# Linear attention and two MLPs on one Trainium2 core: the key-value products of two head pairs in one PSUM tile

## The chip, the cores and the metric

The kernel runs on one core of a Trainium2 chip. The metric is the device time of one execution in microseconds (us); lower is better. Several executions of the kernel before were timed, and one more was recorded by the hardware profiler.

## What is computed

Linear attention, and behind it two MLPs, all in float32 in and out:

```
kv  = einsum('bhsd,bhse->bhde', k, v)         # 8 batches, 8 heads, 576 x 64
o   = einsum('bhsd,bhde->bhse', q, kv)
o   = o / sqrt(mean(o*o, -1) + 1e-6) * g_norm
x   = o, heads side by side: 4608 tokens x 512
x   = leaky_relu(x @ w_in_1) @ w_out_1        # 512 -> 2048 -> 512
out = relu(x @ w_in_2)**2 @ w_out_2
```

## The kernel before

**Stages.** The tokens are nine blocks of 512. The first product of the first MLP (`gemm1`, L522) goes over block j and over m = 0 to 15, a column strip of 128 of the hidden layer: twelve matmuls of 128x512 each into one of four PSUM banks, as each operand is a high and a low part. One such (j, m) is called a slot here; there are 144, numbered 16*j + m. The attention of block j + 1 is done in the slots of block j. The other three products come after that, in a second, longer stage which the change doesn't touch.

**Order.** The order of the work is written out by hand: a list `prog` of steps is made first (L767 to L939) and then played (L993), and each step issues its instructions in that order on its engines, which run them in order. `attention_steps` (L498) gives the steps of a block to slots. For each head pair p (two heads, 0 to 3) it has `kv` (the product of a batch), `a` (the transpose of q, tile `qtps`), `b` (q times kv, tile `ops`), `s` and `t` (sums of squares, tile `ssps`), `c` and `d` (the norm). From block 2 on the head pairs stand four slots apart, and behind a pair's `a` come its `b` two slots later, `s` four, `t` and `c` five and `d` six slots later; `kv` has the slot of `a`. In a slot the steps on weights come first, then the eviction `leaky` of the slot before (L537, which also sends out stores that are due, `tick`, L242), then `gemm1`, then the attention.

**The product of one head pair** is `do_kv` (L349): ten matmuls (five chunks of the sequence, three of 128 rows and two of 96, for two heads) of 64x64 into the two diagonal quarters of a PSUM tile 128 wide, `kvps`. The trace has two rows of each, one per pass. Two copies on ScalarE (L371) then take the high part to the tile `kv`, and two subtractions on VectorE (L374) the low part. Batch 0 is done ahead of slot 0 (L367); batches 1 to 7 make 28 such steps. Six `kv` tiles are used in turn.

**Loads.** `load_kv` (L334) takes two tiles, for k and v of a head pair, and issues four DMAs on the queue of SyncE. `pump` (L976) issues loads ahead of need: a list of `kv` and weight loads, in the order in which the program uses them, goes out as long as at most ten tiles (`LD_BUFS`) are held; `kv` takes two, a weight one, and the head of the list holds up what is behind it. The tiles come free at the step `kv` or `join`.

**Tiles.** Nearly all large tiles come from one list of 44 (`take_big`, `give_big`, L130): the oldest free one is taken. A tile that is sent to DRAM is given back when its store is issued (L242), so the next user's first write waits until that DMA has landed. Such stores are the prepared weights (`whS`, `whA` and others, written on ScalarE at L269 and on GpSimd at L270), and they share the queue of SyncE with all loads.

**PSUM in the attention.** `at_tile` (L327) gives banks 4 to 7 in turn while `gemm1` uses 0 to 3.

Of the kernel before, what the change touches and what calls it, by code (L numbers as in the profile page):

```python
# [11 lines left out]
F32R = mybir.dt.float32r  # L12
U32 = mybir.dt.uint32
AF = mybir.ActivationFunctionType
ALU = mybir.AluOpType
# [3 lines left out]
def tile_linear_attention_two_mlps(  # L19
# [26 lines left out]
    nc = tc.nc  # L46
    B, H, S, D = q.shape
# [6 lines left out]
    P = 128  # L54
    KC = DM // P
    NM = DFF // P
    NP = H // 2

    SCH = ((P, 3), (96, 2))
    SC = sum(n for _, n in SCH)  # L60
# [5 lines left out]
    LD_BUFS, Q_BUFS, KV_BUFS = 10, 4, 6  # L66
# [27 lines left out]
    const = ctx.enter_context(tc.tile_pool(name="const", bufs=1))  # L94
# [7 lines left out]
    ps = ctx.enter_context(tc.tile_pool(name="ps", bufs=1, space=bass.MemoryType.PSUM))  # L102
    dram = ctx.enter_context(tc.tile_pool(name="dram", bufs=1, space=bass.MemoryType.DRAM))

    f32 = lambda t: t.bitcast(F32)
# [4 lines left out]
    eps = const.tile([P, 1], F32, name="eps")  # L110
    eps2 = const.tile([P, 1], F32, name="eps2")
    gneg = const.tile([P, 1], F32, name="gneg")
    kv_t = [const.tile([P, 2, P], F32R, name=f"kv{n}") for n in range(KV_BUFS)]
    x2_d = [dram.tile([KC, P, TB], F32, name=f"x2_{n}") for n in range(NT // TB)]


# [13 lines left out]
    def take_big(shape, dtype, name):  # L130
        n = big_free.pop(0)
        return big.tile(shape, dtype, tag=f"s{n}", name=name), n

    def give_big(*ns):
        big_free.extend(ns)
# [4 lines left out]
    def psum(n, name):  # L140
        return ps.tile([P, TB], F32, tag=f"b{n}", name=name)
# [176 lines left out]
    kv_raw = {}  # L318
# [8 lines left out]
    def at_tile(w, name):  # L327

        at_n[0] += 1
        return psum(at_n[0] % 8 if spare else 4 + at_n[0] % 4, name)[:, :w]  # L330

    x_t = {}

    def load_kv(b, p):  # L334
        tiles = []
        for n, x in enumerate((k, v)):
            name = f"{'kv'[n]}_raw{b}_{p}"
            a, slot = take_big([P, 2, SC, D], F32, name)
            t0 = c0 = 0
            for r, c in SCH:  # L340
                (nc.scalar if n and b == 0 and p else nc.sync).dma_start(
                    out=a[:r, :, c0:c0 + c, :].rearrange("p h c d -> p h (c d)"),
                    in_=x[b, 2 * p:2 * p + 2, t0:t0 + r * c].rearrange("h (p c) d -> p h (c d)", c=c),
                )
                t0, c0 = t0 + r * c, c0 + c
            tiles.append((a, slot))
        kv_raw[b, p] = tiles

    def do_kv(b, p):  # L349
        (kt, k_slot), (vt, v_slot) = kv_raw.pop((b, p))  # L350
        ps = at_tile(P, f"kvps{b}_{p}")
        for c, n in enumerate(n for n, times in SCH for _ in range(times)):
            for h in range(2):
                r = slice(h * D, (h + 1) * D)
                nc.tensor.matmul(
                    out=ps[r, r],
                    lhsT=kt[:n, h, c, :],
                    rhs=vt[:n, h, c, :],
                    start=(c == 0),
                    stop=(c == SC - 1),  # L360
                )
        give_big(k_slot, v_slot)
        t = kv_t[(b * NP + p) % KV_BUFS]
        if b == 0:
            for h in range(2):
                r = slice(h * D, (h + 1) * D)
                nc.vector.tensor_copy(out=kvf_t[p][r, r], in_=ps[r, r])  # L367
            return
        for h in range(2):
            r = slice(h * D, (h + 1) * D)  # L370
            nc.scalar.activation(out=t[r, 0, r], in_=ps[r, r], func=AF.Copy)  # L371
        for h in range(2):
            r = slice(h * D, (h + 1) * D)
            nc.vector.tensor_tensor(  # L374
                out=t[r, 1, r], in0=ps[r, r], in1=f32(t[r, 0, r]), op=ALU.subtract
            )

    def split_kv(p):
# [117 lines left out]
    kv_done = set()  # L496

    def attention_steps(j, pace, a, b_, s, c, d):  # L498
        steps = {}

        def add(n, *st):
            steps.setdefault(n, []).append(st)

        for p in range(NP):
            at0 = int(pace * p)
            for b in range(j * TB // S, (j * TB + TB - 1) // S + 1):
                if (b, p) not in kv_done:
                    kv_done.add((b, p))
                    add(at0 - (j == 0), "kv", b, p)
            add(at0 + a, "a", j, p)  # L510
            add(at0 + b_, "b", j, p)
            add(at0 + s, "s", j, p)
            add(at0 + c, "t", j, p)
            add(at0 + c, "c", j, p)
            add(at0 + d, "d", j, p)
        return steps
# [250 lines left out]
    with tc.manual_schedule():  # L767

        prog = [("const",), ("gn",), ("x", 0)]
        steps = attention_steps(0, 1, 0, 1, 2, 2, 3)  # L770
        jobs = [(0, m, 0) for m in range(NM)]
        for at0 in (3, 5, 6):
# [41 lines left out]
        for s, (j, m) in enumerate(slots):  # L814
            if m == 0 and j + 1 < NB:
                at0, pace = (s - 5, 4) if j else (s, 4)
                put(s, "x", j + 1)
                lags = (2, 4, 5, 6) if j else (1, 2, 2, 3)
                for n, sts in attention_steps(j + 1, pace, 0, *lags).items():
                    for st in sts:  # L820
                        put(at0 + n, *st)
# [44 lines left out]
        u = 0  # L866
        at_slot(t2 - 28, "cap", 21)
        at_slot(t2 - 27.9, "want", (1, 0), 0, NSLOT // 2)
        for x, (half, z) in enumerate(insts):
            t0 = t2 + NPR * u  # L870
            pairs = [(n,) for n in range(half * NPAIR // 2, (half + 1) * NPAIR // 2)]
            if len(SETS[z]) == 1:
                pairs = [pairs[0] + pairs[1], pairs[2] + pairs[3]]
            again = x + 1 < len(insts) and insts[x + 1][1] == z
            if not (x and insts[x - 1][1] == z):
# [4 lines left out]
                for y, (kind, name) in enumerate(todo):  # L880
                    at0 = t0 - lead + 0.7 * y
                    if kind in ("oh", "ol"):
                        nth = [PRODUCTS[p][1] for p in ORDER].index(name)
                        if nth >= EARLY:
                            at0 = max(at0, t0 - 6.6 + 2 * (nth - EARLY) + (0.8 if kind == "ol" else 0))
                    elif name == "T4":
                        at0 = t0 - lead + 0.7 * y
                        at0 = max(at0, t0 - 6.6 + 2 * (4 - EARLY) + 0.9)
# [10 lines left out]
            for y, mine in enumerate(pairs):  # L899
                free = y == len(pairs) - 1 and not again  # L900
                for n in range(NPR):
                    at0 = t2 + NPR * u + 2 * n
                    at_slot(at0, "f", u, z, mine, n, free)
                    c = {2: "C11", 5: "C22", 4: "C21", 3: "C12"}.get(ORDER[n])
# [44 lines left out]
        def drop_pairs(ps):  # L949
# [7 lines left out]

        do = {
            "const": constants, "gn": scale_g, "x": x_tiles, "kv": do_kv,
            "a": stage_a, "b": stage_b, "s": stage_s, "t": stage_t, "kvs": split_kv, "lo": relieve, "c": stage_c, "d": stage_d, "mlp": spare.clear,  # L960
            "scale": scale_w, "join": join_w, "w": split_w, "g1": gemm1, "lk": leaky,
# [3 lines left out]
        }  # L965
        load = {
            "kv": (load_kv, 0, 2), "scale": (load_w, 0, 1), "a": (load_q, 1, 1)
        }
        free_by = {"kv": "kv", "join": "scale", "a": "a"}
        free = [LD_BUFS, Q_BUFS]  # L970
        queue = [
            [(x, st) for x, st in enumerate(prog) if st[0] in load and load[st[0]][1] == n]
            for n in range(2)
        ]

        def pump():  # L976
            while True:
                n = min(
                    (n for n in range(2) if queue[n] and load[queue[n][0][1][0]][2] <= free[n]),
                    key=lambda n: queue[n][0][0], default=None,  # L980
                )
                if n is None:
                    break
                kind, *args = queue[n].pop(0)[1]
                free[n] -= load[kind][2]
                load[kind][0](*args)


# [1 line left out]
        nc.vector.memset(eps, EPS)  # L990
        nc.scalar.activation(out=eps2, in_=eps, func=AF.Abs_reciprocal_sqrt)
        pump()
        for kind, *args in prog:  # L993
            do[kind](*args)
            if kind in free_by:
                _, n, tiles = load[free_by[kind]]
                free[n] += tiles
                pump()


# [30 lines left out]
```

## Time and profile before

| | us |
|---|---|
| median of 3 timed runs (1619.87 to 1621.56) | 1620.13 |
| the profiled execution | 1621.47 |
| its span, first to last instruction | 1619.4 |
| TensorE busy | 1580.0 |
| VectorE busy | 1218.4 |
| ScalarE busy | 768.0 |
| GpSimd busy | 181.0 |

In the rows, PE is TensorE's matmuls, PEld its weight loads, DVE VectorE, ACT ScalarE, POOL GpSimd, and SPq the queue on which SyncE issues DMAs. `out<-in` names the tiles. A bracket at the end of a row gives the idle time of the engine ahead of it and what ended that. The stage with attention reaches from about 31 us (slot 0) to about 548 us.

### The profile page before, as it was taken

To read this page: it belongs to the slowest core of one execution; us is meant where nothing else is said; L and a number is where in the kernel's file an instruction comes from. 1 tells how busy PE (TensorE), PEld (TensorE's weight loads), DVE (VectorE), ACT (ScalarE), POOL (GpSimd) and SP (SyncE) were. 2 spreads that over 40 slices of the span, in tenths; PEclk is the share of its full clock that TensorE was granted. 3 is DMA by queue.
4 is the path that set the end of the run, shared out by engine and by line. 5 is a ranking of instruction groups with operands and counts; after the bars stand their busy time and mean duration, and the time that the engine had idled before them with its cause. 6 is when DMAs were issued, how large, how long until landed. Compare 5 with 4: busy or idle time off the path is not lost. (4 is left out here: it accounts for less than half of the span.)

```text
span 1619.4 us, 27835 instructions
## 1 busy us (share of the span) xinstructions
PE 1580.0 (98%) x10500; PEld 1424.8 (88%) x10500; DVE 1218.4 (75%) x1912; ACT 768.0 (47%) x1435; POOL 181.0 (11%) x208
## 2 busy tenths in 40 slices
PE   5999999999999999999999999999999999999999
PEld 3788877887878899999999988888888999999998
DVE  5967877877773588887778777748886777777776
ACT  4756666565563344444444444534444344444443
POOL 0004444353442000000000000000000000000000
PEclk8999999999999999999999999999999999999999
DMA  9879999999869944444446654574459833344342
GB/s 231 254 210 283 336 288 314 293 301 345 300 232 328 363 132 132 131 131 131 130 132 226 224 177 160 181 255 155 157 169 348 309 130 131 131 131 131 130 133 83
DMA packets 248934, 338.44 MB, mean 209 GB/s; under 512 B 54752, under 2 KB 179680, under 8 KB 248800
## 3 DMA queue, kind: packets, MB, share of 16 engines
q1 hardware_dynamic: 247200, 335.78, 63.3%
q8 instruction: 83, 1.36, 0.3%
q10 hardware_dynamic: 1600, 0.89, 0.2%
q14 instruction: 51, 0.42, 0.1%
HBM read 198.18 MB, written 138.41 MB: 208 GB/s over the span
## 5 line engine op out<-in xcount | busy, mean ns | idle before, releaser
L527 PE MATMUL hps<-xh,w 128*128 128x512 f32 x1152 | 382.7, 400 | 10.5 <-ACT w L213 5.7
L527 PEld LDWEIGHTS hps<-xh,w 128*128 128x128 f32 x1152 | 218.3, 190 | 61.8 <-DVE w L214 6.9
L527 PE MATMUL hps<-xl,w 128*128 128x512 f32 x576 | 226.5, 393 | 0.0
L527 PEld LDWEIGHTS hps<-xl,w 128*128 128x128 f32 x576 | 109.6, 190 | 22.1 <-issue 1.0
L539 ACT ACTIVATE h<-hps 128x512 f32<-128x512 f32 x144 | 84.2, 589 | 20.6 <-DMA g<-h 16.0
L633 DVE TENSOR_TENSOR h_C<-aps,u 128x512 f32<-128x512 f32 x72 | 49.6, 688 | 45.1 <-PE aps L654 44.9
L633 DVE TENSOR_TENSOR u<-bps,p 128x512 f32<-128x512 f32 x72 | 49.5, 688 | 33.7 <-ACT p L664 20.8
L443 POOL TENSOR_TENSOR sqs<-sqo,sqs 128x512 fp32r<-128x512 f32 x28 | 43.3, 1547 | 189.6 <-DVE sqs L442 170.0
L664 ACT ACTIVATE p<-aps 128x512 f32<-128x512 f32 x36 | 21.3, 591 | 73.3 <-PE aps L654 73.3
L471 DVE SCALAR_TENSOR_TENSOR sqo<-ssps,sqo 128x512 f32<-128x512 f32 x36 | 24.9, 691 | 40.1 <-ACT sqo L470 39.8
L654 PE MATMUL aps<-op_B21h,w 128*128 128x512 f32 (+1 forms) x160 | 52.1, 375 | 1.1 <-ACT p L664 1.1
L654 PE MATMUL bps<-op_T4h,w 128*128 128x512 f32 (+1 forms) x160 | 51.3, 369 | 0.7 <-DVE u L633 0.7
L654 PE MATMUL aps<-op_B22h,w 128*128 128x512 f32 (+1 forms) x160 | 51.1, 368 | 0.0
L654 PE MATMUL bps<-op_T2h,w 128*128 128x512 f32 (+1 forms) x160 | 51.0, 368 | 0.0
L654 PE MATMUL bps<-op_T3h,w 128*128 128x512 f32 (+1 forms) x160 | 51.0, 368 | 0.0
L654 PE MATMUL aps<-op_B11h,w 128*128 128x512 f32 (+1 forms) x160 | 51.0, 368 | 0.0
L654 PE MATMUL aps<-op_T1h,w 128*128 128x512 f32 (+1 forms) x160 | 51.0, 368 | 0.0
L633 DVE TENSOR_TENSOR u<-ps,p 128x512 f32<-128x512 f32 x18 | 12.5, 692 | 50.9 <-ACT p L729 50.9
L671 ACT ACTIVATE h_C<-aps 128x512 f32<-128x512 f32 x36 | 21.6, 599 | 61.0 <-issue 31.1
L685 DVE SCALAR_TENSOR_TENSOR h_C<-h_C 128x512 f32<-128x512 f32 x72 | 49.1, 682 | 0.0
L181 DVE SCALAR_TENSOR_TENSOR w_raw<-w_raw 128x512 uint32<-128x512 uint32 x64 | 47.3, 739 | 2.2
L195 DVE SCALAR_TENSOR_TENSOR wt<-wt,w_raw 128x512 uint32<-128x512 uint32 x64 | 44.3, 693 | 2.2
(1417 smaller groups left out, 4174.4 us busy)
## 6 DMA issues: line engine op xcount, KB each, us to landing
g_raw<-g SPq DMA_DIRECT2D x144, 512.0 KB, 5.2
w<-w SPq DMA_DIRECT2D x84, 512.0 KB, 6.7
g<-h SPq DMA_DIRECT2D x144, 256.0 KB, 4.9
g<-h_C SPq DMA_DIRECT2D x144, 256.0 KB, 2.5
w_raw<-in_moe_w_in_dram SPq DMA_DIRECT2D x32, 512.0 KB, 5.3
w_raw<-in_moe_w_out_dram SPq DMA_DIRECT2D x32, 512.0 KB, 5.4
w<-whS SPq DMA_DIRECT2D x64, 256.0 KB, 4.7
x_raw<-x SPq DMA_DIRECT2D x32, 512.0 KB, 6.5
```

The lines of the kernel that those rows point to most:

```text
L181: nc.vector.scalar_tensor_tensor(out=lower, in0=lower, scalar=29, in1=upper, op0=ALU.logical_shift_right, op1=ALU.bitwise_or,)
L195: nc.vector.scalar_tensor_tensor(out=t, in0=t, scalar=3, in1=lower, op0=ALU.logical_shift_left, op1=ALU.bitwise_or,)
L443: nc.gpsimd.tensor_tensor(out=sqs[:, 1], in0=sqo[:, 0], in1=f32(sqs[:, 0]), op=ALU.subtract)
L471: nc.vector.scalar_tensor_tensor(out=z, in0=ps, scalar=EPS, in1=z, op0=ALU.add, op1=ALU.mult)
L527: nc.tensor.matmul(out=ps, lhsT=w[:, wh, c * P:(c + 1) * P], rhs=x_t[j][xh, c // 2][0][:, c % 2, :], start=(c == 0 and y == 0), stop=(c == ...
L539: nc.scalar.activation(out=h, in_=h_ps.pop((j, m)), func=AF.Prelu, alpha=0.01)
L633: nc.vector.tensor_tensor(out=t, in0=x, in1=y, op=ALU.add)
L654: nc.tensor.matmul(out=ps[:, p], lhsT=w[:, wh, c, :], rhs=t[xh][:, c, :], start=(fresh and p == 0 and c == 0 and y == 0), stop=(p == len(p ...
L664: nc.scalar.activation(out=p1, in_=ps, func=AF.Copy)
L671: nc.scalar.activation(out=h, in_=ps, func=AF.Relu)
L685: nc.vector.scalar_tensor_tensor(out=h, in0=h, scalar=0.0, in1=h, op0=ALU.max, op1=ALU.mult)
```

## The change

`do_kv` and `load_kv` take one or two head pairs. With two, the matmuls of both stand one after the other in one PSUM tile 256 wide, and each of the four copy-out instructions takes both pairs: 64 partitions by 2 x 64 elements. The two `kv` tiles become halves of one. The step has the slot of the first pair, so the second pair's product is made four slots earlier. Its load asks for four tiles at once and issues eight DMAs. Batch 0 and the first two pairs of batch 2 stay single. So 13 steps have two pairs and two have one, in place of 28.

```diff
-    kv_t = [const.tile([P, 2, P], F32R, name=f"kv{n}") for n in range(KV_BUFS)]
+    kv_g = [const.tile([P, 2, 2, P], F32R, name=f"kv{n}") for n in range(KV_BUFS // 2)]
+    kv_t = [kv_g[n // 2][:, n % 2] for n in range(KV_BUFS)]
...
-    def load_kv(b, p):
+    def load_kv(b, *pairs):
+        for p in pairs:
+            load_kv_pair(b, p)
+
+    def load_kv_pair(b, p):
...
-    def do_kv(b, p):
-        (kt, k_slot), (vt, v_slot) = kv_raw.pop((b, p))
-        ps = at_tile(P, f"kvps{b}_{p}")
...
+    def do_kv(b, *pairs):
+        ps = at_tile(P * len(pairs), f"kvps{b}_{pairs[0]}")
+        for u, p in enumerate(pairs):
+            (kt, k_slot), (vt, v_slot) = kv_raw.pop((b, p))
+            for c, n in enumerate(n for n, times in SCH for _ in range(times)):
+                for h in range(2):
+                    nc.tensor.matmul(
+                        out=ps[h * D:(h + 1) * D, u * P + h * D:u * P + (h + 1) * D],
+                        lhsT=kt[:n, h, c, :],
+                        rhs=vt[:n, h, c, :],
+                        start=(c == 0),
+                        stop=(c == SC - 1),
+                    )
+            give_big(k_slot, v_slot)
...
+        t = kv_g[(b * NP + pairs[0]) % KV_BUFS // 2][:, pairs[0] % 2:pairs[-1] % 2 + 1]
+        by_u = ps.rearrange("k (u f) -> k u f", u=len(pairs))
         for h in range(2):
             r = slice(h * D, (h + 1) * D)
-            nc.scalar.activation(out=t[r, 0, r], in_=ps[r, r], func=AF.Copy)
+            nc.scalar.activation(out=t[r, :, 0, r], in_=by_u[r, :, r], func=AF.Copy)
         for h in range(2):
             r = slice(h * D, (h + 1) * D)
             nc.vector.tensor_tensor(
-                out=t[r, 1, r], in0=ps[r, r], in1=f32(t[r, 0, r]), op=ALU.subtract
+                out=t[r, :, 1, r], in0=by_u[r, :, r], in1=f32(t[r, :, 0, r]), op=ALU.subtract
             )
...
                 if (b, p) not in kv_done:
-                    kv_done.add((b, p))
-                    add(at0 - (j == 0), "kv", b, p)
+                    pairs = (p, p + 1) if b and (b, p // 2) != (2, 0) else (p,)
+                    kv_done.update((b, x) for x in pairs)
+                    add(at0 - (j == 0), "kv", b, *pairs)
...
+        def tiles_of(kind, *args):
+            return load[kind][2] * (len(args) - 1 if kind == "kv" else 1)
```

`pump` and the loop that plays the list count tiles with `tiles_of`.

## Rows read from the trace of the kernel before

**Rows 1.** The page, part 1: busy time of each engine, its share and instructions.

```profile
PE 1580.0 (98%) x10500; PEld 1424.8 (88%) x10500; DVE 1218.4 (75%) x1912; ACT 768.0 (47%) x1435; POOL 181.0 (11%) x208
```

**Rows 2.** Waits of PE, whole span: us in total, times, longest.

```profile
PE ssps L454 <- DVE sqs L442: 8.7, 6, 3.4
```

**Rows 3.** Timeline of PE, slots 103 and 107: start us, us, instruction, count, idle before.

```profile
413.70 0.60 PE L405 MATMUL qtps<-ident,q_raw 128*128 128x128 f32 x4
414.23 0.80 PE L355 MATMUL kvps<-v_raw,k_raw 128*64 128x64 f32 x20
414.96 0.50 PE L527 MATMUL hps<-xh,w 128*128 128x512 f32 x1
415.30 0.39 PE L527 MATMUL hps<-xl,w 128*128 128x512 f32 x1
...
427.46 0.60 PE L405 MATMUL qtps<-ident,q_raw 128*128 128x128 f32 x4
427.82 0.48 PE L527 MATMUL hps<-xh,w 128*128 128x512 f32 x1
428.13 0.39 PE L527 MATMUL hps<-xl,w 128*128 128x512 f32 x1
```

**Rows 4.** Timeline of PE cut at 140 us, so only eight of twenty show.

```profile
139.74 0.45 PE L355 MATMUL kvps<-v_raw,k_raw 128*64 128x64 f32 x8
```

**Rows 5.** Tile kv: duration ns min/median/max, first and last start us, forms.

```profile
L371 ACT ACTIVATE kv<-kvps x56: 198/219/242, 40.0 to 417.0; 64x64 fp32r<-64x64 f32 x56
L374 DVE TENSOR_TENSOR kv<-kvps,kv x56: 204/218/230, 41.4 to 417.7; 64x64 fp32r<-64x64 f32 x56
L380 ACT ACTIVATE kv<-kvf x4: 294/296/311, 40.5 to 41.1; 128x128 fp32r<-128x128 f32 x4
L381 DVE TENSOR_TENSOR kv<-kvf,kv x4: 285/285/293, 41.8 to 42.5; 128x128 fp32r<-128x128 f32 x4
```

**Rows 6.** Timeline of PE, slots 63 to 71 and 91 to 99.

```profile
264.28 0.80 PE L355 MATMUL kvps<-v_raw,k_raw 128*64 128x64 f32 x20
280.36 0.79 PE L454 MATMUL ssps<-sqs,ones 128*128 128x512 f32 x1 [3.09 <-DVE sqs L442]
...
297.72 0.80 PE L355 MATMUL kvps<-v_raw,k_raw 128*64 128x64 f32 x20
...
366.07 0.80 PE L355 MATMUL kvps<-v_raw,k_raw 128*64 128x64 f32 x20
383.06 0.80 PE L454 MATMUL ssps<-sqs,ones 128*128 128x512 f32 x1 [3.38 <-DVE sqs L442]
...
400.47 0.80 PE L355 MATMUL kvps<-v_raw,k_raw 128*64 128x64 f32 x20
```

**Rows 7.** Windows: length, PE PEld DVE ACT POOL busy (count), PEclk, DMA share, GB/s.

```profile
283.00:293.00 10.00, 10.00 (x44) 8.15 (x41) 9.05 (x17) 5.99 (x15) 2.93 (x3) 0.81 0.99 296
...
386.00:396.00 10.00, 10.00 (x39) 8.20 (x40) 9.13 (x17) 5.95 (x14) 3.43 (x4) 0.84 0.99 305
```

**Rows 8.** Timeline of ACT around the two stalls.

```profile
267.75 0.60 ACT L412 ACTIVATE qhl<-qtps 128x512 fp32r<-128x512 f32 x1 [3.02 <-DMA w<-whS]
272.84 0.42 ACT L269 ACTIVATE whA<-wt 128x256 fp32r<-128x256 f32 x1 [1.97 <-DMA w<-whS]
...
374.91 0.42 ACT L269 ACTIVATE whA<-wt 128x256 fp32r<-128x256 f32 x1 [2.94 <-DMA w<-whS]
```

**Rows 9.** Timeline of SyncE's queue ahead of the first stall.

```profile
256.25 2.94 SPq L393 DMA_DIRECT2D q_raw<-in_q_dram  x4
...
264.09 1.42 SPq L341 DMA_DIRECT2D k_raw<-in_k_dram  x2
265.61 0.95 SPq L341 DMA_DIRECT2D v_raw<-in_v_dram  x2
266.65 2.45 SPq L248 DMA_DIRECT2D w<-whS  x2
```

**Rows 10.** The page, part 6: DMA issues, KB each, median us from issue to landing.

```profile
w<-whS SPq DMA_DIRECT2D x64, 256.0 KB, 4.7
```

More of the change, by code (lines that the diff above doesn't have):

```diff
@@ L347, in load_kv @@
         kv_raw[b, p] = tiles
-    def do_kv(b, p):
-        (kt, k_slot), (vt, v_slot) = kv_raw.pop((b, p))
-        ps = at_tile(P, f"kvps{b}_{p}")
[L352 to L363, printed above, removed]
+    def do_kv(b, *pairs):
[12 more added lines that the diff above has]
+            give_big(k_slot, v_slot)
         if b == 0:
+            p, = pairs
             for h in range(2):
@@ L978, in pump @@
                 n = min(
-                    (n for n in range(2) if queue[n] and load[queue[n][0][1][0]][2] <= free[n]),
+                    (n for n in range(2) if queue[n] and tiles_of(*queue[n][0][1]) <= free[n]),
                     key=lambda n: queue[n][0][0], default=None,
@@ L984, in pump @@
                 kind, *args = queue[n].pop(0)[1]
-                free[n] -= load[kind][2]
+                free[n] -= tiles_of(kind, *args)
                 load[kind][0](*args)
@@ L995, in tile_linear_attention_two_mlps @@
             if kind in free_by:
-                _, n, tiles = load[free_by[kind]]
-                free[n] += tiles
+                n = load[free_by[kind]][1]
+                free[n] += tiles_of(free_by[kind], *args)
                 pump()
```

## The prediction

> **What bounds the kernel.** I read the busy line first: TensorE is busy 98% of the span, VectorE 75%, ScalarE 47% [rows 1]. So what a change is worth is read from TensorE: instructions that leave its stream, and stretches in which it stands still. The waits of TensorE come next. In the stage that the change touches, the largest sum is for one cause: the matmul of the sums of squares waits for VectorE's cast `sqs`, 8.7 us in six times, the longest 3.4 [rows 2]. The timeline then shows two things about which the argument goes: what one key-value step costs TensorE [rows 3, 4], and where the two long stalls stand, in slots 67 and 95 [rows 6].
>
> **The change, part by part.**
>
> *Fewer changes between the two kinds of matmul.* In slot 107 no `kv` step follows the transposes: from their start to the next `gemm1` matmul it takes 427.82 - 427.46 = 0.36 us, and 0.31 to the one after, 0.67 in all. In slot 103 there is one: 414.23 - 413.70 = 0.53, then 0.73, then 0.34 us, 1.60 in all [rows 3]. So a step of 20 rows costs 0.93 us on TensorE. How fast the rows flow inside a step: eight end after 0.45 us, twenty after 0.80 [rows 4, 3], so (0.80 - 0.45) / 12 = 0.029 us each and 0.58 for twenty. The other 0.93 - 0.58 = 0.35 us is the price of going into the group and out of it, and it falls once for every step that is joined to another: 13 * 0.35 = 4.5 us. In this stage nothing but the stalls stands between TensorE's matmuls, so this comes off the end. The other bound is nought: inside one step the rows go from chunks of 128 rows to chunks of 96 without a visible cost, but the way back, which the second pair adds, is in no row. I take 4.5, as one direction is seen to be free. Two of the 13 lie in slots 0 to 8, where VectorE prepares weights and may set the pace; there the copies below save as much, so the term stands.
>
> The rows' 0.35 us can be set against a rule. The Trainium skill's TensorEngine Tiling, section Key Properties, says that changing the tiling mode drains TensorE, and its TensorE: Matmul & The Clock Gate, Part 2, puts the way of the last column through the array at about 128 cycles. An estimate from that page's figure is 2 * 128 / 2.4 GHz = 0.11 us for a step, 1.4 us for 13, and the forecast would lie 3.1 us higher. The trace agrees that there is a price and shows a larger one.
>
> *Fewer copies.* Four instructions of 219 ns on ScalarE become two, likewise four of 218 on VectorE. A copy of 2 x 64 elements is in no row; it lies between one of 64 and one of 128 over all partitions, 219 to 296 ns on ScalarE, 218 to 285 on VectorE [rows 5]. I take the upper ends, since two runs of 64 are 128 elements: 4 * 219 - 2 * 296 = 0.28 us a step on ScalarE, 4 * 218 - 2 * 285 = 0.30 on VectorE, about 3.7 and 3.9 us for 13. Both engines work beside TensorE, and I count nothing for it. If that cover went, because they came late for `sqs`, the saving would help.
>
> *The second pair earlier.* Its product is made four slots sooner, and read no sooner than before. The first pair's copies now wait for the second pair's twenty rows, 0.58 us, and `b` reads them two slots later. A slot lasts (414.23 - 400.47) / 4 = 3.44 us [rows 6, 3], so that is covered six times over; without this cover `b` would stall by 0.58. PSUM: the `kv` tile takes one turn in place of two, so the kinds of tile shift through banks 4 to 7, but following the turns, from slot 18 on each bank comes round again after four slots or more, as before. I count nothing.
>
> *The loads.* The list holds ten tiles, and a pair of pairs asks for four at its head. Following the plan, from block 3 on each goes out in slot 8n + 3 when the pair before gives up its four, and is used eight slots later: 27 us against a landing of some 5 [rows 10]. Data are not late. What changes is that eight `k` and `v` DMAs follow one another on SyncE's queue. Four take 1.42 + 0.95 = 2.4 us to issue [rows 9], so eight take 4.8 where 2.4 stood in one place and 2.4 in another. The number of DMAs is the same.
>
> *The turn of the tiles.* This is the largest term. The two stalls have one source. ScalarE waited 3.02 and 1.97 us, and in the other case 2.94, for tiles whose weight store had not landed [rows 8]; behind it the squares came late, so `sqs`, so TensorE. Each cost more than its 3.09 or 3.38 us, as the granted clock then was 0.81 and 0.84 over the next ten us [rows 7], that is, part of them was spent at 1.2 GHz. From one `kvps` to the second next is 297.72 - 264.28 = 33.4 and 400.47 - 366.07 = 34.4 us, against 2 * 13.76 = 27.5 undisturbed [rows 6, 3]: 5.9 and 6.9, on average 6.4 us for a stall.
>
> Why these tiles? I followed the list of 44 tiles through the plan, each take and each return. Between slots 16 and 127 the old order has 23 takes for ScalarE or VectorE (the x tiles aside, which are written later) of a tile that a store gave back no more than two slots before. The waits in rows 8 are three of them: `qhl` in 63, `whA` in 64 and in 92. In the new order 10 are left, and none of these three: the `qhl` tile comes from TensorE's `t`, `whA` in 64 from a store three slots back, in 92 from none. So both stalls lose their source. Against that, slot 52 takes for `whA` a tile that a store gave back only one slot before, with 3.44 us for a landing of 4.7 [rows 10]. With the longer burst of loads ahead of some stores I expect that one stall of the same size comes in, between nought and two or more. That makes 2 * 6.4 - 6.4 = 6.4 us off.
>
> **Sum.** 4.5 + 6.4 = 10.9 us off. The profiled execution took 1621.47, of which 1619.4 are the span, so it would come to 1610.6; it stands 1.3 us over the median of the runs, 1620.13, and against that the forecast is 1609.2, say 1609 us.
>
> **The rivals.**
>
> *No stall at all.* Both sources go and slot 52 costs nothing, since ScalarE stood 272.84 - 265.01 = 7.8 us behind the start of slot 64 (264.28 + 0.73) [rows 8, 6, 3], and a landing of 4.7 in place of 3.44 leaves it far less late. For it speaks the count of 10 against 23; against it that the ages alone don't set the waits. 1620.1 - 4.5 - 12.8 = 1602.8 us; with the four small waits of rows 2 gone too, about 2 us less.
>
> *Stalls as before, elsewhere.* Only the changes of kind are saved: 1620.1 - 4.5 = 1615.6 us. The plan repeats against the weights every 28 slots and the new loads every eight, so the stalls may just move.
>
> *The joining saves nothing on TensorE.* If the way back from 96 to 128 rows costs what the exit cost, and the stalls stay, it is 1620 us, no change.
>
> *Slower: the burst on SyncE's queue.* In slot 8n + 3 the queue gets four `q` DMAs (2.94 us), eight `k` and `v` (4.8) and two to four weights: over 8 us of issuing for a slot of 3.44. Already before, the store that ScalarE waited for went out at 266.65, right behind four such loads [rows 9]. With twice as many, each store behind a burst goes out 2.4 us later, and tiles of three slots' age become late too. There are ten such bursts, from slot 19 to 91. It decides from three stalls: 1620.1 - 4.5 + 6.4 = 1622.0, and with four 1628.4 us.
>
> **How the numbers follow.** One stall (the forecast) 0.36; none 0.28; two as before 0.18; nothing saved 0.06; three or more 0.12. Faster by over 0.2% (3.2 us, about what a measurement of this kernel can tell from no change) means below 1616.9. The first two cases lie below it, the third by 1.3 us only, so I give it two thirds there and the rest to "same": faster 0.36 + 0.28 + 0.11 = 0.75, same 0.07 + 0.06 = 0.13, slower 0.12. The range goes from the case of no stall with part of the small waits gone, 1601, to that of no saving and two stalls, 1620.5; it leaves out the burst with its 0.12 and a little at the low end.
>
> **What would show it.** Each step right: `kvps` rows in 13 groups of 40, with 1.16 us of flow and one step's exit and entry; from the transposes to the second `gemm1` matmul 1.60 + 0.58 = 2.18 us in one slot and 0.67 in the other, in place of 1.60 in each; copies of 64 x 128 near 296 and 285 ns; no wait of TensorE near slots 67 and 95, and at most one of over 3 us, near slot 55. It is wrong if a group of 40 takes 2.5 us or more; if ScalarE waits for stores right behind the bursts, in slots 8n + 4 to 8n + 7, three times or more; or if long stalls of `ssps` stand where they stood.

## The result and the profile after

| | before | after |
|---|---|---|
| median of 6 runs each, us | 1620.36 (1619.41 to 1624.45) | 1632.74 (1629.34 to 1634.44) |
| the profiled execution, us | 1621.47 | 1634.44 |
| its span, us | 1619.4 | 1632.2 |

The ratio is 1.0066 with a 95% interval of 1.0055 to 1.0077: slower by 10.7 us; the medians are 12.4 us apart, and below both measures are given where they differ. The forecast was 1609, with a range up to 1620.5. Both the sign and the range were wrong.

The page of the changed kernel, part 1, against [rows 1]:

```profile
PE 1579.2 (97%) x10500; PEld 1423.8 (87%) x10500; DVE 1214.0 (74%) x1886; ACT 762.9 (47%) x1409; POOL 181.2 (11%) x208
```

ScalarE and VectorE have 26 instructions fewer each, two for each of the 13 joined steps. No engine works longer to speak of, so the 13 us by which the span grew are idle time. The step itself came out as forecast. Timeline of PE after, one joined step (compare [rows 3]):

```profile
113.06 0.60 PE L412 MATMUL qtps<-ident,q_raw 128*128 128x128 f32 x4
113.59 1.39 PE L360 MATMUL kvps<-v_raw,k_raw 128*64 128x64 f32 x40
114.91 0.50 PE L535 MATMUL hps<-xh,w 128*128 128x512 f32 x1
115.24 0.39 PE L535 MATMUL hps<-xl,w 128*128 128x512 f32 x1
```

From the transposes to the second `gemm1` matmul it is 115.24 - 113.06 = 2.18 us, to the hundredth what the prediction asked for. The copies, tile `kv` after (duration in ns min/median/max, first and last start, forms), against [rows 5]:

```profile
L378 ACT ACTIVATE kv<-kvps x30: 204/272/275, 40.9 to 415.4; 64x128 fp32r<-64x128 f32 x26, 64x64 fp32r<-64x64 f32 x4
L381 DVE TENSOR_TENSOR kv<-kvps,kv x30: 208/278/295, 41.5 to 417.5; 64x128 fp32r<-64x128 f32 x26, 64x64 fp32r<-64x64 f32 x4
```

They take 272 and 278 ns by the median, under the 296 and 285 that were assumed. So the change does what it says, and the loss lies elsewhere.

**Where TensorE waits now.** Waits of PE, whole span, after (us in total, times, longest), against [rows 2]:

```profile
PE ssps L461 <- DVE sqs L449: 9.2, 8, 3.0
PE ops L437 <- ACT qhl L419: 7.8, 3, 4.6
...
PE hps L535 <- DVE w L215: 5.6, 4, 2.5
PE hps L535 <- ACT h L547: 5.1, 2, 4.3
```

The second and the fourth of these lines are new: TensorE waits for ScalarE itself, twice for over 4 us. What holds up ScalarE shows in its own timeline, after, 95 to 405 us (the bracket is the idle time ahead of the row and what ended it), against [rows 8]:

```profile
131.34 0.60 ACT L547 ACTIVATE h<-hps 128x512 f32<-128x512 f32 x1 [1.57 <-DMA g<-h]
159.24 0.42 ACT L270 ACTIVATE whS<-ws 128x256 fp32r<-128x256 f32 x1 [7.90 <-DMA w<-whA]
189.10 0.60 ACT L547 ACTIVATE h<-hps 128x512 f32<-128x512 f32 x1 [3.35 <-DMA g<-h]
220.75 0.60 ACT L547 ACTIVATE h<-hps 128x512 f32<-128x512 f32 x1 [3.61 <-DMA g<-h]
250.34 0.42 ACT L270 ACTIVATE whA<-wt 128x256 fp32r<-128x256 f32 x1 [4.09 <-DMA w<-whS]
309.64 0.60 ACT L547 ACTIVATE h<-hps 128x512 f32<-128x512 f32 x1 [4.13 <-DMA g<-h]
369.17 0.42 ACT L270 ACTIVATE whS<-ws 128x256 fp32r<-128x256 f32 x1 [6.75 <-DMA w<-whA]
403.04 0.60 ACT L419 ACTIVATE qhl<-qtps 128x512 fp32r<-128x512 f32 x1 [7.74 <-DMA w<-whA]
```

Every one is a wait for a store, of a prepared weight or of `g<-h`. (Two shorter ones, 2.19 us at 234.50 and 1.85 at 297.19, are left out.) Before there were six waits of ScalarE on DMAs in this stretch, 13.5 us in all, the three of [rows 8] among them, none over 3.0; now there are ten with 43.2 us, and single ones last up to 7.9. What stood ahead of the first long one on SyncE's queue, timeline of SP after:

```profile
140.64 3.05 SPq L400 DMA_DIRECT2D q_raw<-in_q_dram  x4
143.79 1.06 SPq L346 DMA_DIRECT2D k_raw<-in_k_dram  x2
144.94 0.91 SPq L346 DMA_DIRECT2D v_raw<-in_v_dram  x2
145.90 0.96 SPq L346 DMA_DIRECT2D k_raw<-in_k_dram  x2
146.96 0.91 SPq L346 DMA_DIRECT2D v_raw<-in_v_dram  x2
147.97 0.88 SPq L167 DMA_DIRECT2D w_raw<-in_moe_w_out_dram  x2
148.94 3.54 SPq L249 DMA_DIRECT2D w<-whA  x4
152.57 0.94 SPq L249 DMA_DIRECT2D g<-h  x1
```

This is a train: four loads of q, eight of k and v, two whole weights of 512 KB, and only then the four stores of `whA`. ScalarE gets the tile of one of them at 159.24, 10.3 us after the first of the four was issued. There are ten such trains from 113 to 392 us, one about every eight slots, with two to four weights each, and each of the eight waits above ends 8 to 12 us after the last weight of one was issued. The weights and the stores behind them also take longer to land. DMA issues in the window 95 to 400 us (count, KB each, median us from issue to landing), the kernel before:

```profile
w<-whA SPq DMA_DIRECT2D x48, 256.0 KB, 4.5
w_raw<-in_moe_w_out_dram SPq DMA_DIRECT2D x21, 512.0 KB, 5.3
w_raw<-in_moe_w_in_dram SPq DMA_DIRECT2D x16, 512.0 KB, 4.8
```

and the same after:

```profile
w<-whA SPq DMA_DIRECT2D x48, 256.0 KB, 6.4
w_raw<-in_moe_w_out_dram SPq DMA_DIRECT2D x18, 512.0 KB, 7.2
w_raw<-in_moe_w_in_dram SPq DMA_DIRECT2D x16, 512.0 KB, 7.7
```

Not everything lands later: the medians of the stores `w<-whS` (4.7 to 4.8) and `g<-h` (4.7 to 4.9) hardly move, and the loads of k and v land sooner. What grows is the tail. Taken one by one from the traces, none of the 200 such stores (`whS`, `whA`, `whT`, `g<-h`) in this window took more than 7.4 us before, and 42 of 189 take over 7.5 after. The stores that end the eight waits above took 7.5 to 9.2 us from their issue, those that ended the waits of before 4.7 to 5.9. So what holds up ScalarE arises in good part after the issue of the store.

How full the DMA engines are in this stage is in the windows view, 95 to 400 us (length; busy us and count of PE, PEld, DVE, ACT, POOL; PEclk; DMA share; GB/s). The kernel before:

```profile
95.00:400.00 305.00, 296.80 (x1696) 243.12 (x1695) 226.63 (x378) 184.25 (x410) 128.22 (x139) 0.98 0.94 297
```

and after:

```profile
95.00:400.00 305.00, 287.33 (x1668) 234.82 (x1666) 215.52 (x345) 172.34 (x373) 122.25 (x133) 0.99 0.87 280
```

TensorE is busy 9.5 us less in the same stretch, and the DMA engines went from 94% to 87%: late stores hold up ScalarE, then TensorE, and so the next loads too. The granted clock is the same (0.98 and 0.99), so it has no part in it. Nor are the DMA engines full while a train goes out. The train shown, and the time from there to the next one, windows after:

```profile
140.64:148.85 8.21, 8.21 (x73) 7.07 (x74) 4.23 (x10) 6.81 (x17) 5.06 (x7) 1.00 0.75 205
148.85:171.90 23.05, 22.18 (x137) 18.02 (x136) 18.35 (x28) 12.77 (x28) 9.41 (x9) 1.00 0.95 317
```

During nine of the ten trains the share is 0.53 to 0.84 (in the last 0.99), and between them 0.91 to 1.01.

Slot by slot, by the starts of `ssps`, the kernel after lies 1.1 us behind at slot 15, 2.5 at slot 47, 4.6, 6.7 and 10.0 at slots 51, 55 and 59 and 10.6 at slot 63. It is only 5.7 behind at slot 68, as the first old stall is gone, then 13.4 at slot 87, 5.7 again at slot 96, as the second is gone, and 12.9 at slot 99, after the wait that ends at 403.04. It ends the stage 12.6 behind. So both old stalls did go, as forecast, and more came in.

### The profile page after: what moved, and what is told of

Read it like the earlier page. It is cut to its first block, busy times and chain, and to the rows that moved or that the text cites. A ratio compares the mean times of both kernels' runs of the same rounds, so it can differ in the third digit from the quotient of the medians.

```text
span 1632.2 us, 27749 instructions
## 1 busy us (share of the span) xinstructions
PE 1579.2 (97%) x10500; PEld 1423.8 (87%) x10500; DVE 1214.0 (74%) x1886; ACT 762.9 (47%) x1409; POOL 181.2 (11%) x208
## 5 line engine op out<-in xcount | busy, mean ns | idle before, releaser
L420 DVE TENSOR_TENSOR qhl<-qtps,qhl 128x512 fp32r<-128x512 f32 x32 | 22.0, 688 | 47.7 <-ACT qhl L419 42.3
L641 DVE TENSOR_TENSOR u<-ps,p 128x512 f32<-128x512 f32 x18 | 12.4, 692 | 51.3 <-ACT p L737 51.3
L679 ACT ACTIVATE h_C<-aps 128x512 f32<-128x512 f32 x36 | 21.6, 599 | 61.2 <-issue 31.2
```

The costliest lines, as they stand in the source:

```text
L420: nc.vector.tensor_tensor(out=t[:, 1], in0=ps, in1=f32(t[:, 0]), op=ALU.subtract)
L641: nc.vector.tensor_tensor(out=t, in0=x, in1=y, op=ALU.add)
L679: nc.scalar.activation(out=h, in_=ps, func=AF.Relu)
```

## The experiments

The theories: **(A)** the long train of loads, and that weights are let out right behind it, makes stores late; **(B)** the turn of the tiles is worse than was counted, that is, tiles are taken too soon after a store; **(C)** the joined product itself costs something on TensorE or in PSUM. Each of four groups (e1 to e4; e5, e6, e9 and e10; e11 to e14; e15 to e17) shared its runs of the kernel before, whose medians were 1621.49, 1621.85, 1622.33 and 1621.23 us. Medians and ratios differ by up to some 3 us when two versions are compared across groups, so both are given.

| kernel | median us | ratio to before (95%) |
|---|---|---|
| after | 1632.74 | 1.0066 (1.0055 to 1.0077) |
| e1 after, one pair per load | 1623.33 | 1.0013 (1.0002 to 1.0025) |
| e2 before, two pairs per load | 1620.32 | 0.9999 (0.9988 to 1.0009) |
| e3 after, passing over | 1625.22 | 1.0036 (1.0023 to 1.0049) |
| e4 before, passing over | 1613.55 | 0.9959 (0.9944 to 0.9974) |
| e5 as e3, six `h` tiles | 1625.68 | 1.0017 (1.0007 to 1.0028) |
| e6 as e3, one pair per load | 1619.57 | 0.9984 (0.9970 to 0.9998) |
| e9 after, late return | 1621.36 | 0.9991 (0.9981 to 1.0001) |
| e10 as e3, late return | 1616.04 | 0.9958 (0.9944 to 0.9973) |
| e11 as e10, loads spread | 1613.61 | 0.9942 (0.9929 to 0.9956) |
| e12 as e11, no passing over | 1620.58 | 0.9993 (0.9984 to 1.0002) |
| e13 as e2, passing over | 1618.04 | 0.9975 (0.9966 to 0.9984) |
| e14 e4 again | 1613.22 | 0.9948 (0.9935 to 0.9961) |
| e15 as e3, at most 8 tiles held | 1617.49 | 0.9974 (0.9964 to 0.9984) |
| e16 after, at most 8 tiles held | 1618.53 | 0.9980 (0.9970 to 0.9989) |
| e17 as e3, v on ScalarE's queue | 1628.08 | 1.0047 (1.0029 to 1.0066) |

**e1: joined products, loads asked for one pair at a time.**

```diff
-            [(x, st) for x, st in enumerate(prog) if st[0] in load and load[st[0]][1] == n]
+            [
+                (x, st2) for x, st in enumerate(prog) if st[0] in load and load[st[0]][1] == n
+                for st2 in ([(*st[:2], p) for p in st[2:]] if st[0] == "kv" else [st])
+            ]
```

> The products stay joined, but each head pair's k and v are a load of their own again (two tiles, four DMAs), as before the change. Theory A (the loads: four tiles asked for at once go out as eight DMAs in a row and hold up the weight stores on SyncE's queue): the stalls of the changed kernel go, at most 2 of over 2 us stay, and with 4.5 us saved on TensorE the time is 1608 to 1618 us. Theory B (only the turn of the 44 tiles, which falls by accident): the turn is another one again, so the time may be anything from 1605 to 1635. Theory C (the joined step itself, that is its place four slots earlier and its longer stretch on TensorE, makes the engines late): no better than the changed kernel, 1630 to 1635 us.

**e2: the kernel before, but its loads of two pairs together.** Entries `kv b, p` and `kv b, p + 1` of the load list become one that needs four tiles, as in the change; products and copies stay single.

> The kernel before, with its single products in their old slots, but the loads of two head pairs asked for together (four tiles, eight DMAs). Theory A: slower than before by 8 to 20 us, 1628 to 1640 us, with ScalarE waiting for weight stores issued behind the eight DMAs. Theory B: anything from 1610 to 1640. Theory C: as before, 1618 to 1623 us.

e1 took 1623.3: over nine of the 12.4 us between the two kernels (8.6 of 10.7 by the ratios) go away when only the request for loads is split. The time still lies above the 1608 to 1618 of theory A, and ScalarE still waits three times for 5.5 to 6.0 us for stores of prepared weights, so B is not out. e2 took 1620.3, no change, where A had 1628 to 1640 and C 1618 to 1623. So e1 puts the larger part of the loss on the loads, which speaks against C, but by e2 a long burst of k and v alone does not do it: something must go with it, or the burst's price is hidden in e2 (see e13).

**e3 and e4: tiles just stored are passed over.** A take that is not a load skips tiles whose store was issued less than four slots ago, if there are others. e3 does it to the changed kernel, e4 to the kernel before.

```diff
-    def take_big(shape, dtype, name):
-        n = big_free.pop(0)
+    def take_big(shape, dtype, name, load=False):
+        at = 0
+        if not load:
+            old = [x for x, n in enumerate(big_free) if stored_at.get(n, -9) <= slot_n[0] - 4]
+            at = old[0] if old else 0
+        n = big_free.pop(at)
```

> The changed kernel, but a tile that a store gave back less than four slots ago is passed over for ScalarE's and VectorE's outputs, and the oldest other free tile is taken (loads still take the oldest). Loads, products and their order are unchanged. If the waits for stored tiles are what the time went to (A and B alike), ScalarE's waits for weight stores fall from five of over 2 us to one at most, and the time falls to 1610 to 1620 us; what is left is waits of the eviction for its own store. If the stalls have another source (C, or the eviction's five buffers alone), it stays at 1628 to 1635 us.

> The kernel before with the same passing over of tiles that a store has just given back. If its two stalls (5.9 and 6.9 us with the slower clock behind them) have the source that the prediction gave them, both go and the time is 1604 to 1612 us. If not, it stays at 1618 to 1623 us.

e4 gained 6.6 us by its ratio and 8 by the medians and so lies between its two ranges; no wait of ScalarE for a store is left in 95 to 500 us, and TensorE's wait for `sqs` is halved. Waits of PE in that window, e4:

```profile
PE ssps L464 <- DVE sqs L452: 4.4, 7, 1.5
```

That is about what the two old stalls cost together: slot by slot, e4 gains 4.9 us on before from slot 64 to 72 and 6.3 from slot 92 to 100, and gives 2.3 of it back. The prediction had put 12.8 on them. e3 gained about as much against after (4.9 by the ratios, 7.5 by the medians), also between its ranges, and still stands some 12 us above e4. All waits of ScalarE for weight stores are gone, and one kind is left. Waits of ACT from 95 to 400 us, e3:

```profile
ACT h L557 <- DMA g<-h: 24.3, 12, 4.7
```

So B explains as much in the kernel before as in the changed one, and not the difference of the two.

**e5: as e3, with six `h` tiles in place of five** (and 43 tiles in the list, which gives up one).

```diff
-    NBIG = 44
+    NBIG = 43
...
-    hp = ctx.enter_context(tc.tile_pool(name="hp", bufs=5))
+    hp = ctx.enter_context(tc.tile_pool(name="hp", bufs=6))
```

> The changed kernel with passing over, and a sixth buffer for the tile h that the eviction writes, with 43 large tiles in place of 44 to make room. In the changed kernel with passing over, ScalarE waited some ten times for an h tile whose store stood behind the loads. If those waits are what the 12 us over the kernel before with passing over went to, a buffer more takes them away: 1609 to 1616 us. If they are only a symptom (late weights, late data), it stays at 1622 to 1628.

1625.7 against 1625.2; by the ratios it could be 0.2% better. The waits for `h` in the same window fall from 24.3 us in twelve to 12.7 in five, and the time hardly moves. More room for `h` brings back little or nothing: that wait is a symptom.

**e6: as e3, with the loads of e1.**

> Joined products, a load for each head pair of its own (two tiles), and the passing over. A2: the four tiles still come back at once, so pairs of loads and weights may still go out as one train at some places; 1608 to 1618 us. C: 1620 or more.

1619.6, that is 5.7 us off e3 (8.4 by the ratios), between the ranges of A2 and C. Splitting the request helps here too, but it does not reach e4. The joined step still gives back four tiles at once, so that a request and two weights still go out together, as at 143.31 to 146.34 us in its trace.

**e9 and e10: two of the four tiles count as free later.** In the changed kernel the joined step returns the places of both pairs at once, and `pump` then lets out whatever stands at the head of its list. Here the second pair's places are counted free only at its `a`, four slots later. e9 is the changed kernel with that alone, e10 has e3's passing over too.

```diff
+                if kind == "kv" and len(args) > 2:
+                    held.add((args[0], args[2]))
+                    args = args[:2]
+                if kind == "a" and tuple(args) in held:
+                    ...
+                    free[0] += tiles_of("kv", *args)
```

> The changed kernel, but of the four tiles that a joined step sets free in the count of loads, two are counted free only four slots later, as before the change. Products, copies and the eight DMAs of a joined load stay; what goes is that two to four weights of 512 KB follow the eight in the same slot. Theory A2 (the joined step returns four tiles at once, so the k and v loads and the weights go out as one train, and the stores behind it come late): 8 to 17 us faster than the changed kernel, 1614 to 1624 us, at most two waits of the eviction for its store before slot 130. Theory A1 (the eight DMAs alone): 1628 to 1635. Theory C (the joined step itself): 1628 to 1635.

> The same late return, and the passing over of tiles that a store has just given back. With both sources of lateness gone only the joined products' saving is left against the kernel before with passing over (1613.6 us): A2 says 1613.6 - 4.5 = 1609 us, 1607 to 1613. C says no faster than 1613.6, up to 1625.

e9 took 1621.4, 11 us off after (12 by the ratios), with the products joined and their eight DMAs still in a row. Its queue in the same stretch as the train above, timeline of SP, e9:

```profile
145.26 1.05 SPq L346 DMA_DIRECT2D k_raw<-in_k_dram  x2
146.41 0.91 SPq L346 DMA_DIRECT2D v_raw<-in_v_dram  x2
147.36 0.96 SPq L346 DMA_DIRECT2D k_raw<-in_k_dram  x2
148.42 0.91 SPq L346 DMA_DIRECT2D v_raw<-in_v_dram  x2
149.43 2.23 SPq L249 DMA_DIRECT2D w<-whA  x4
...
152.72 0.64 SPq L167 DMA_DIRECT2D w_raw<-in_moe_w_out_dram  x1
...
156.44 0.93 SPq L167 DMA_DIRECT2D w_raw<-in_moe_w_out_dram  x1
```

The eight loads are there as before, but the stores come next, and the two weights follow one at a time, 3 and 7 us later. So the time is what A2 had said, but not the sign that went with it: the eviction still waits four times for its store (9.0 us, 95 to 400 us), where two at most were expected. e10, at 1616.0, stands 9.2 us below e3 (12.6 by the ratios); it misses the 1607 to 1613 of A2, and e11 shows what is left. So the larger part is neither the joined product nor the eight DMAs, but the weights that four places returned at once let out behind them.

**e11 and e12: as e10, and each pair's load back at its old place** (the second pair's entry is sorted in at its `a`, from batch 2 on). Only the joined product, at its earlier place, is left of the change. e12 is without passing over. **e13** is e2 with passing over, and **e14** is e4 again, beside them.

> Joined products with passing over, and the loads put back to what they were: each head pair's k and v a load of its own in its old place in the list (from batch 2 on), and the second pair's two tiles counted free four slots later. Nothing of the change is left but the joined step. Theory A2 with A1 (all of the rest of the loss stands in the trains of loads): 1608 to 1612 us, 2 to 5 us below the kernel before with passing over, which runs beside it. Theory C (the joined step costs elsewhere what it saves on TensorE): the same as that kernel, within 1.5 us, or slower.

> As the first kernel of this call, without passing over: the joined step alone, with the loads and the turn of the tiles close to what they were. If loads and turn are all that cost, about 4 us below the kernel before, 1614 to 1619 us; the turn of the tiles is not quite the old one, and a stall of 6 us more or less may come with it.

> Single products in their old slots, passing over, and the loads of two pairs asked for together: the price of eight DMAs in a row alone, without the turn of the tiles. A1 (the eight cost something by themselves): 3 to 8 us over the kernel before with passing over. If only the longer train with the weights costs: within 1.5 us of it.

> The kernel before with passing over, once more on this chip, to stand beside the joined one: 1611 to 1616 us by its first runs. All theories say the same of it.

e13 against e14: eight DMAs in a row cost 4.4 us (0.9975 against 0.9948) where products are single; e10 against e11 gives 2.4 by the medians on joined ones. So the zero of e2 was a balance: slot by slot e2 is 4.0 us ahead of before at slot 72, where the first old stall is smaller in its turn of the tiles, and level with it again at slot 88. e12 against before is 0.9993 and not told from no change; 1614 to 1619 had been expected.

e11 against e14 is the worth of the joined product alone, 1613.6 against 1613.2, with intervals that overlap, where 2 to 5 us had been expected. The 4.5 us do show on the way: by the starts of `ssps` slot by slot, e11 is 0.4 us behind at first, then gains 0.35 us with each joined pair, 3.8 by slot 88 and 4.4 by slot 96. Then it gives most of it back. Timeline of ACT, e11:

```profile
381.21 0.60 ACT L557 ACTIVATE h<-hps 128x512 f32<-128x512 f32 x1 [4.08 <-DMA g<-h]
```

and of PE, e11:

```profile
388.06 0.50 PE L471 MATMUL ssps<-sqs,ones 128*128 128x512 f32 x1 [1.57 <-DVE sqs L459]
...
417.09 0.47 PE L471 MATMUL ssps<-sqs,ones 128*128 128x512 f32 x1 [1.56 <-DVE sqs L459]
```

In e14 ScalarE has no wait for a store from 95 to 500 us. At the end of the stage 1.5 us of lead are left, too little for these intervals. So C falls as the cause of the loss: the joined product makes nothing slower. But in the milder form that C had for e11, that the step costs elsewhere what it saves on TensorE, it came true: the product brings next to nothing.

**e15 and e16: at most eight tiles held, not ten.** This too keeps weights from following the train. e15 has passing over, e16 is the changed kernel with this number alone.

```diff
-    LD_BUFS, Q_BUFS, KV_BUFS = 10, 4, 6
+    LD_BUFS, Q_BUFS, KV_BUFS = 8, 4, 6
```

> The changed kernel with passing over, and eight load tiles in place of ten: four for the joined pair leave four, so fewer weights can follow the eight DMAs. If the weights behind the eight are the larger part of the train's cost (9 us between the changed kernel with passing over and the same with late return), 1613 to 1620 us; if not, 1622 to 1628.

> The changed kernel with eight load tiles in place of ten and nothing else. Two tiles more stay in the list, so what ScalarE takes was given back earlier, and the train is shorter: both causes are weakened by one number. 1616 to 1624 us if trains and stored tiles are the causes, 1629 or more if not.

e15 is 7.7 us below e3 (10.0 by the ratios), e16 14.2 below after and 0.2% below the kernel before, both in the range for trains. A second, simpler edit gives back about the same as the late return. The two have one more thing in common than the train: both hold fewer loads in flight. The kernel before with eight tiles was not run, so what that alone is worth stays open; e1, which keeps all ten, gives back over nine us too. The weights of e15 land sooner than after's 7.2 and 7.7 us. DMA issues from 95 to 400 us, e15:

```profile
w_raw<-in_moe_w_out_dram SPq DMA_DIRECT2D x21, 512.0 KB, 5.9
w_raw<-in_moe_w_in_dram SPq DMA_DIRECT2D x16, 512.0 KB, 6.4
```

**e17: as e3, with the v loads from batch 2 on issued on ScalarE's queue.** It asks whether the train is long because SyncE must issue it, or because of what it carries.

```diff
-                (nc.scalar if n and b == 0 and p else nc.sync).dma_start(
+                (nc.scalar if n and (b == 0 and p or b > 1) else nc.sync).dma_start(
```

> [...] If the time on SyncE's queue is what holds up the stores, 4 to 9 us faster than with passing over alone, 1616 to 1621 us. If the bytes on the DMA engines hold them up, 1623 to 1627 us; if ScalarE is held up by issuing, slower than that.

Timeline of SP, e17, its train:

```profile
202.42 2.57 SPq L410 DMA_DIRECT2D q_raw<-in_q_dram  x4
205.04 2.11 SPq L356 DMA_DIRECT2D k_raw<-in_k_dram  x4
207.25 0.87 SPq L177 DMA_DIRECT2D w_raw<-in_moe_w_out_dram  x2
208.16 0.99 SPq L170 DMA_DIRECT2D w_raw<-in_moe_w_in_dram  x2
```

SyncE issues it in 209.15 - 202.42 = 6.7 us, in e3 the same train with its v loads took 8.7. Yet the time is 1628.1, not below e3's 1625.2. Less issuing on SyncE did not help. That fits a limit in what the loads carry. But the time lies above the range given for that, the v loads went out earlier here (196.69 to 200.46 us), and ScalarE has to issue them now, at 0.4 to 2.2 us each on its queue, and may give back what SyncE gains. So the run doesn't settle it.

## Why the prediction was wrong, and where it was right

**Fewer changes between the two kinds of matmul: right on TensorE, not kept.** 2.18 us for a joined step, 0.35 us gained by each. The Trainium skill's TensorEngine Tiling, section Key Properties, has the rule that a change of mode drains the engine; the trace agrees that the change has a price. The 0.11 us that the prediction estimated for it from the Trainium skill's TensorE: Matmul & The Clock Gate, Part 2, was too small: with 0.11 fixed, (0.93 - 0.11) / 20 = 0.041 us would be left for a row, and a joined step would take 0.67 + 0.11 + 40 * 0.041 = 2.42 us against the 2.18 measured. The step failed at "this comes off the end". e11 shows 4.4 us of it at slot 96 and 1.5 at the end of the stage: a TensorE that runs ahead meets the stores, as the row at 381.21 shows.

**Fewer copies, the second pair earlier: right.** The copies take 272 and 278 ns, e11 shows nothing of them in the time, and no wait for a bank appears among TensorE's largest.

**"The loads": wrong; here is the larger half of the miss.** "Data are not late" and "the number of DMAs is the same" both hold, and that the time stays the same does not follow from them. What was left out is that a request for four places, and a step that gives back four, change what goes out together. In place of groups of four the queue gets q, eight of k and v, and two to four weights in one stretch, and the stores right behind them land late. Counted as 0, it measured 2.4 us for the eight in a row (e10 against e11) and 9.2 for the weights behind them (e3 against e10), 12 to 15 in all by medians or ratios.

**"The turn of the tiles": its sources right, its sum wrong.** Both old stalls lost their source as the ages said. But an age in slots is worth something only against a landing time that stays: it was counted against 4.7 us [rows 10], and behind the trains single stores took up to 10 us. With 10 young takes in place of 23, the waits for stored tiles still cost 5 to 7.5 us net after (after against e3), where before's cost 6.6 to 8 (before against e4). So the 6.4 us of gain were 1 or so. Two stalls at 6.4 us each were also too many: both together are worth the 6.6 to 8 us of e4, so part of what one loses is made good later anyway.

These three together are about the miss: about 3 to 4 us of saving not kept, 5 to 6 in the turn, 12 to 15 in the loads, against 10.9 + 10.7 = 21.6 between forecast and result.

**The slower rival** had the place and the sign with a chance of 0.12: waits of ScalarE for stores behind the bursts, three times or more, were to show it, and the eight rows above do. Its price was short, as it counted eight k and v DMAs as the burden, 2.4 us more per burst, and 6.4 us for a stall; it named the two to four weights and gave them no weight of their own. Its end, 1622 to 1628, is still too low. One of its readings was wrong as well: the store of 266.65 [rows 9] ended ScalarE's wait of 1.97 us, while the longer one, of 3.02, was for a store issued at 262.37, ahead of those four loads. And in the chances two thirds of 0.18 are 0.12, not 0.11, which changes nothing.

**What the rows had said.** The windows that were read for the clock [rows 7] give a DMA share of 0.99 at 296 and 305 GB/s in their next two columns. Over the stage it was 0.94 before. In e4, the fastest version on single products, it is 0.96. Windows, 95 to 400 us, e4:

```profile
95.00:400.00 305.00, 301.94 (x1762) 247.88 (x1761) 234.70 (x390) 187.78 (x419) 130.70 (x141) 1.00 0.96 303
```

One reading is that the DMA engines are a second bound close behind TensorE in this stage, so that a transfer moved ahead pushes back the ones behind it. It fits e9, e15, e16 and e17, but it is argued and not shown. Against its simplest form, that the engines are full while a train goes out, stand the windows above: 0.75 at 205 GB/s during the train, 0.95 at 317 GB/s behind it. They allow another: twelve small DMAs in a row, at 0.5 to 0.8 us of issue each, leave the engines part empty, and the weights and stores queue up behind. Whether the bytes or their issue set the price stays open.

## What to carry to other kernels

Before calling a prefetch free because its data come early enough, look at the DMA share of that stage: where it is near 1, as here, ask which store stands behind the loads that are moved, and who writes its tile next. A step that returns several places at once lets out as many loads at once; give the places back one by one, or hold fewer. And let writers pass over tiles that were only just stored: that alone was worth 0.4 to 0.5% here, more than the 4.5 us (0.3%) that the change itself could bring, and e4 and e11 (1613.6 us both) beat both kernels.

## What was not expected of the hardware

Moving a quarter of the train's DMAs to another engine's queue shortened the issuing from 8.7 to 6.7 us and made nothing faster (e17). Holding fewer loads in flight was faster: with eight tiles held in place of ten, 14 us of the changed kernel's time went away. And the median landing time of the same 512 KB loads (`w_in`) went from 4.8 to 7.7 us from one kernel to the other, and was 6.4 in e15, though the loads themselves are the same.
